# TensorE reads w1 through a register-held ring slot; q is scaled by VectorE

## The chip, the cores and the metric

One NeuronCore of a Trainium2 chip runs the kernel. The metric is the device time of one execution in microseconds. An execution counts as fast or slow by its state (a run over 1.5% above the fastest of the same kernel is slow); comparisons below use fast runs. A ratio is the mean time of one kernel's fast runs over the mean of the other's fast runs of the same rounds, with its 95% interval, so it is not quite the ratio of the medians that stand beside it.

Names of engines: PE is TensorE's array (PEld its weight loads, PEq or PEldq its sequencer), DVE is VectorE, ACT ScalarE, POOL GpSimd, SP the engine that issues most input and output transfers (128 of the 164 DMA issues on the page of the kernel before).

## The reference, cut to what matters

```python
# q, k, v: (8 batches, 8 heads, 576 tokens, 64); moe_w1: (8 experts, 512, 1024); moe_w2: (8, 1024, 512)
q_s = softmax(q, axis=-1)                      # per token: this is "q scaled"
k_s = softmax(k, axis=2)                       # over the tokens
x   = einsum(q_s, einsum(k_s, v))              # (8, 576, 512) after joining the heads
e_idx = argmax(x.mean(axis=1) @ w_gate)        # ONE expert for each batch
h   = maximum(x[b] @ w1[e_idx[b]], 0)
out[b] = gate_w[b] * (h @ w2[e_idx[b]])
```

For these inputs the gate chooses the experts 2, 3, 3, 1, 3, 3, 4, 6.

## The kernel before

The batches run one after the other. The expert's weights lie in SBUF in a ring of five slots, `w1_all` and `w2_all`. Batch b owns slot b mod 5. GpSimd loads the expert into that slot, unless one of the other slots already holds it. Which slot holds the weights of batch b is known only at run time (`sidx`). Before, VectorE reads that number into a register and copies the weights into the batch's own slot, so that PE's addresses are constants:

```python
def fetch(b, w_all, part):                     # once per half of w1 and of w2
    if "src" not in seqs[b]:
        seqs[b]["src"] = nc.values_load(seqs[b]["sidx"][0:1, 0:1], engines=[ET.DVE], ...)
    ...                                        # cs, fs: the half
    copy = nc.vector.tensor_copy(
        out=w_all[:, b % NS, cs, fs],
        in_=w_all[:, ds(seqs[b]["src"], 1), cs, fs].rearrange("p o c f -> p (o c) f"),
    )
def moe(b):
    w1_sb, w2_sb = w1_all[:, b % NS], w2_all[:, b % NS]
    for fc in range(NF):                       # 8 blocks of 128 rows of h
        for c in range(ND):                    # 4 matmuls of 512 tokens
            nc.tensor.matmul(phm, lhsT=w1_sb[:, c, fsl], rhs=xt[:, c, 0:SM], ...)
        for c in range(ND):                    # 4 matmuls of the last 64 tokens
            nc.tensor.matmul(pht[...], lhsT=w1_sb[:, c, fsl], rhs=xt[:, c, SM:S], ...)
        ...
        yield                                  # attention work of later batches is put in here
    ...                                        # w2 stage: 4 x 8 matmuls of 512 columns, 16 of 256
```

A "block" below is one turn of the `fc` loop: 8 weight loads and 8 matmuls. The w1 stage of a batch is eight blocks, the w2 stage follows. The attention work of the batches to come is put between the blocks, up to batch 6; batch 7 has none.

The softmax here doesn't subtract the row's maximum and nothing guards it: scores larger than these inputs give would overflow.

## Time and profile before

| | before |
|---|---|
| time, median of 3 runs | 215.05 us (213.42 to 219.71; the last counts as slow) |
| profiled span | 213.7 us, mean granted clock 0.919 |
| PE busy | 176.0 us (82%) |
| one block with nothing between (batch 7) | 0.98 us |

L181 is PE's transpose of the scaled q: of the 7.6 us that PE idles ahead of it, 3.0 are ended by GpSimd. L219 forms x; PE idles 2.7 us ahead of it.

### The profile page before, as it was taken

Reading aid. Unit: us, or ns where it says so; the run is one execution under the profiler, and the core shown is the slowest. Engines: PE = TensorE matmul, PEld = TensorE weight load, DVE = VectorE, ACT = ScalarE, POOL = GpSimd, SP = SyncE. Lnnn points to the kernel's source line nnn. Section 1 sums busy time; section 2 is a strip of 40 time slices with the busy share of each in tenths; the row PEclk is TensorE's granted clock in tenths of the full one; section 3 lists DMA queues with packets and bytes.
Section 4 is the critical chain, followed back from the end, with each engine's and each line's share of the span. In section 5 each row is a group of like instructions: output and inputs, shape, how many; then the busy total and the mean of one; then the engine's idle time right before and its main releaser. Section 6 shows DMA issues by size and latency. Waiting matters only on the chain.

```text
span 213.7 us, 4597 instructions
## 1 busy us (share of the span) xinstructions
PE 176.0 (82%) x1703; PEld 94.3 (44%) x1703; DVE 119.0 (56%) x365; ACT 113.3 (53%) x177; POOL 62.2 (29%) x70
## 2 busy tenths in 40 slices
PE   6357499996999379797498999999777979999990
PEld 6344345443545135433244454535343535545540
DVE  0757935137697977994455757974755365222000
ACT  2776854672974418651266728653582334546541
POOL 2143600630266330373026230730084302300000
PEclk9965559999999859999969999999996999999999
DMA  6999899999998998999999595814379751999044
GB/s 187 379 390 369 123 206 298 230 217 297 398 389 253 395 348 276 336 323 240 275 244 324 158 328 119 300 36 114 76 110 200 141 123 48 160 186 270 1 113 110
DMA packets 28582, 48.55 MB, mean 227 GB/s; under 512 B 2960, under 2 KB 10128, under 8 KB 28560
## 3 DMA queue, kind: packets, MB, share of 16 engines
q1 hardware_dynamic: 19472, 37.76, 53.5%
q0 software_dynamic: 8544, 10.49, 30.1%
q8 instruction: 13, 0.21, 0.4%
q10 hardware_dynamic: 544, 0.02, 0.1%
q14 instruction: 9, 0.07, 0.1%
HBM read 61.88 MB, written 9.44 MB: 334 GB/s over the span
## 4 chain that ended last, share of the span: by engine, by line
PE 43%; DMA 25%; DVE 19%; issue 5%; POOL 3%; ACT 1%; DVEq 1%; POOLq 0%; ACTq 0%
PE mm L421 19%; DMA w_all<-in_moe_w_dram 17%; PE mm L402 15%; DVE w_all L385 7%; DMA v_in<-in_v_dram 5%; DVE qs L142 4%; DMA wg_sb<-in_moe_w_gate_dram 3%; PE kv L160 2%; PE mm L436 2%; PE x L219 2%; PE ht L407 2%; DVE kv L170 2%; DVE qt L189 2%; DVE xt L230 1%; PE kv L181 1%
## 5 line engine op out<-in xcount | busy, mean ns | idle before, releaser
L402 PE MATMUL mm<-xt,w_all 128*128 128x512 f16 x256 | 69.9, 405 | 12.8 <-DVE w_all L385 12.8
L411 ACT ACTIVATE hsb<-mm 128x512 f16<-128x512 f32 x64 | 37.8, 596 | 45.0 <-PE mm L402 44.5
L421 PE MATMUL mm<-w_all,hsb 128*128 128x512 f16 x256 | 60.6, 383 | 0.4 <-DMA w_all<-in_moe_w_dram 0.3
L428 ACT ACTIVATE osb<-mm,gate 128x512 f32<-128x512 f32 x32 | 22.0, 687 | 37.3 <-PE mm L421 31.0
L385 DVE COPY w_all<-w_all 128x2048 f16 x28 | 29.5, 1052 | 14.0 <-DMA w_all<-in_moe_w_dram 13.7
L402 PEld LDWEIGHTS <-w_all 128*128 128x128 f16 x256 | 21.4, 102 | 34.8 <-DVE w_all L385 14.5
L145 POOL TENSOR_TENSOR eq<-eq,qsi 128x1152 f16<-128x1152 f16 x13 | 28.0, 2152 | 26.6 <-DVE qsi L144 25.5
L421 PEld LDWEIGHTS <-hsb 128*128 128x128 f16 x256 | 23.3, 98 | 26.2 <-issue 0.8
L230 DVE CUSTOM_DVE_ANT_0 xt<-x,ones_f 128x576 f16<-128x576 f32 x26 | 19.3, 743 | 17.1 <-PE x L220 17.1
L315 POOL DMA_DIRECT2D w_all<-in_moe_w_dram x18 | 8.2, 455 | 66.1 <-DMA w_all<-in_moe_w_dram 24.8
L142 DVE TENSOR_REDUCE qs<-eq 128x18 f32<-128x1152 f16 x16 | 21.5, 1343 | 10.1 <-ACT eq L124 10.1
L132 POOL CAST va<-v_in 128x1152 f16<-128x1152 f32 x14 | 17.7, 1261 | 24.7 <-DMA v_in<-in_v_dram 24.6
L407 PEld LDWEIGHTS <-w_all 128*128 128x128 f16 x256 | 17.0, 101 | 17.1 <-issue 3.3
L124 ACT ACTIVATE eq<-q_in 128x1152 f16<-128x1152 f32 x16 | 18.5, 1159 | 2.3 <-DMA q_in<-in_q_dram 2.3
L136 ACT ACTIVATE ek<-k_in 128x1152 f16<-128x1152 f32 x16 | 18.6, 1161 | 1.1 <-DMA k_in<-in_k_dram 1.1
L407 PE MATMUL ht<-xt,w_all 128*128 128x64 f16 x256 | 18.6, 197 | 0.0
L219 PE MATMUL x<-qt,kv 128*128 128x512 f16 x32 | 14.0, 438 | 2.7 <-DVE kv L170 0.8
L168 DVE RECIPROCAL icv<-kv 128x1 f32<-128x1 f32 x30 | 4.8, 162 | 18.7 <-PE kv L181 18.2
L160 PE MATMUL kv<-va,ek 64*128 64x129 f16 x270 | 11.7, 230 | 3.3 <-POOL va L132 2.1
L160 PEld LDWEIGHTS <-ek 64*128 64x128 f16 x288 | 10.1, 102 | 8.2 <-issue 6.6
L181 PE MATMUL kv<-ident,eq 64*128 64x64 f16 x270 | 7.3, 196 | 7.6 <-POOL eq L145 3.0
L170 DVE SCALAR_TENSOR_TENSOR kv<-kv,icv,blkmask 128x128 f16<-128x128 f32 x30 | 10.5, 351 | 1.1
(80 smaller groups left out, 133.8 us busy)
## 6 DMA issues: line engine op xcount, KB each, us to landing
w_all<-in_moe_w_dram POOLq DMA_DIRECT2D x30, 512.0 KB
q_in<-in_q_dram SPq DMA_DIRECT2D x16, 576.0 KB, 6.6
k_in<-in_k_dram SPq DMA_DIRECT2D x16, 576.0 KB, 9.2
v_in<-in_v_dram SPq DMA_DIRECT2D x16, 576.0 KB, 9.1
out_dram<-osb SPq DMA_DIRECT2D x64, 128.0 KB, 5.5
w_all<-in_moe_w_dram POOLq DMA_DIRECT2D x4, 256.0 KB
out_dram<-osb_t SPq DMA_DIRECT2D x16, 64.0 KB, 2.2
wg_sb<-in_moe_w_gate_dram ACTq DMA_DIRECT2D x2, 8.0 KB, 5.3
```

Of the source, the lines that this page charges most:

```text
L124: nc.scalar.activation(out=eq.rearrange("p j n d -> p n j d"), in_=ins.pop((n, "q")), func=AF.Exp)
L136: nc.scalar.activation(out=ek.rearrange("p j n d -> p n j d"), in_=ins.pop((n, "k")), func=AF.Exp)
L142: nc.vector.tensor_reduce(out=qs, in_=eq, op=ALU.add, axis=AX.X)
L145: eng.tensor_tensor(out=eq, in0=eq, in1=qsi.unsqueeze(3).to_broadcast([128, J, 2, Dh]), op=ALU.mult,)
L160: nc.tensor.matmul(kps[g][:, 0:129], lhsT=ek[r, j], rhs=va[r, j], start=(j == 0), stop=(j == J - 1),)
L230: nc.vector.tensor_tensor_reduce(out=xt[:, c, :], in0=px[:, 0:S], in1=ones_f32.to_broadcast([128, S]), scale=1.0, scalar=0.0, op0=ALU.mult ...
L385: copy = nc.vector.tensor_copy(out=w_all[:, b % NS, cs, fs], in_=w_all[:, ds(seqs[b]["src"], 1), cs, fs].rearrange("p o c f -> p (o c) f"),)
L402: nc.tensor.matmul(phm, lhsT=w1_sb[:, c, fsl], rhs=xt[:, c, 0:SM], start=(c == 0), stop=(c == ND - 1),)
L407: nc.tensor.matmul(pht[:, fc * ST:(fc + 1) * ST], lhsT=w1_sb[:, c, fsl], rhs=xt[:, c, SM:S], start=(fc == 0 and c == 0), stop=(fc == NF - ...
L411: nc.scalar.activation(out=hsb[:, fc, 0:SM], in_=phm, func=AF.Relu)
L421: nc.tensor.matmul(po, lhsT=hsb[:, fc, st * 128:st * 128 + 128], rhs=w2_sb[:, fc, :], start=(fc == 0), stop=(fc == NF - 1),)
L428: nc.scalar.mul(osb, po, gate)
```

## The change

The intent: PE takes w1 from whichever slot holds it, so the w1 copies and PE's waits for them go. The slot number sits in a PE register, and each weight load's address is worked out from it. Only w2 is still copied. The scaling of q moves to VectorE, which has lost half its copies. Cut to its core:

```diff
-            at(t - 4.25, scale_q, n, nc.gpsimd)
+            at(t - 3.25, scale_q, n, nc.vector)
...
+    def find(b):
+        seqs[b]["src"] = nc.values_load(seqs[b]["sidx"][0:1, 0:1], engines=[ET.PE], ...)
+
+    def w1_of(b, c, cols):
+        if b == 0:
+            return w1_all[:, 0, c, cols]
+        return w1_all[:, ds(seqs[b]["src"], 1), c, cols].rearrange("p o f -> p (o f)")
...
-                    phm, lhsT=w1_sb[:, c, fsl], rhs=xt[:, c, 0:SM],
+                    phm, lhsT=w1_of(b, c, fsl), rhs=xt[:, c, 0:SM],
...
-                    pht[...], lhsT=w1_sb[:, c, fsl], rhs=xt[:, c, SM:S],
+                    pht[...], lhsT=w1_of(b, c, fsl), rhs=xt[:, c, SM:S],
...
-            at(NU * b - 1 + 0.5 * part, fetch, b, w1_all, part)
-            at(NU * b + 4 + part, fetch, b, w2_all, part)
+        at(NU * b - 3, find, b)
+            at(NU * b + 4 + part, fetch, b, part)
-    places = [(15, 25), (30, 35), (41, 46), (58, 64), (74, 80), (91, 97)]
+    places = [(15, 25), (31, 36), (42, 47), (58, 64), (74, 80), (91, 97)]
```

A rule had to change with it: a batch that reuses an expert no longer holds w1 in its own slot, so it isn't entered in the list of slots to reuse. (That part of the diff is left out here.)

More of the change, by code (lines that the diff above doesn't have):

```diff
@@ L80 @@
     hist = consts.tile([1, 8], FP32)
-    nc.vector.memset(hist, -1.0)
+    nc.vector.memset(hist, 0.0)
     held = consts.tile([1, 8], FP16)
@@ L109 @@
     out_p = out.rearrange("b (p j) d -> b p j d", j=J)
-    ins, halves, seqs, issued, copies = {}, {}, {}, {}, {}
+    ins, halves, seqs, issued, uses = {}, {}, {}, {}, {}
     def load(n, names="qkv"):
@@ L278, in gate_step @@
             same = gat_pool.tile([1, 8], FP32, name="same")
-            nc.vector.tensor_tensor(
-                out=same, in0=hist, in1=eidx[0:1, 0:1].to_broadcast([1, 8]), op=ALU.is_equal
+            nc.vector.scalar_tensor_tensor(
+                out=same, in0=hist, scalar=-1.0, in1=eidx[0:1, 0:1].to_broadcast([1, 8]),
+                op0=ALU.add, op1=ALU.is_equal,
             )
@@ L291, in gate_step @@
             nc.vector.max_index(out=sidx, in_max=top, in_values=score)
-        nc.vector.tensor_copy(out=hist[:, slot:slot + 1], in_=eidx[0:1, 0:1])
+        if b:
+            loaded = gat_pool.tile([1, 1], FP32, name="loaded")
+            nc.vector.tensor_single_scalar(out=loaded, in_=top[:, 0:1], scalar=1.0, op=ALU.is_equal)
+            nc.vector.scalar_tensor_tensor(
+                out=hist[:, slot:slot + 1], in0=eidx[0:1, 0:1], scalar=1.0, in1=loaded,
+                op0=ALU.add, op1=ALU.mult,
+            )
+        else:
+            nc.vector.tensor_single_scalar(
+                out=hist[:, slot:slot + 1], in_=eidx[0:1, 0:1], scalar=1.0, op=ALU.add
+            )
         gone = (b + 2) % NS
-        nc.vector.memset(hist[:, gone:gone + 1], -1.0)
+        nc.vector.memset(hist[:, gone:gone + 1], 0.0)
         nmx = gat_pool.tile([1, 1], FP32, name="nmx")
@@ L321, in gate_step @@
         for load_inst in issued[b]:
-            for copy in copies.get(b - 1, ()):
-                apart(load_inst, copy)
+            for op in uses.get(b - 1, ()):
+                apart(load_inst, op)
     def apart(first, second):
@@ L372, in gate_spread, with fetch @@
         seqs[b]["gate"] = gate
-    def fetch(b, w_all, part):
-        if "src" not in seqs[b]:
-            seqs[b]["src"] = nc.values_load(
+    def find(b):
+        seqs[b]["src"] = nc.values_load(
+            seqs[b]["sidx"][0:1, 0:1], engines=[ET.PE], min_val=0, max_val=NS - 1,
+            skip_runtime_bounds_check_because=IN_RANGE,
+        )
+    def w1_of(b, c, cols):
+        if b == 0:
+            return w1_all[:, 0, c, cols]
+        return w1_all[:, ds(seqs[b]["src"], 1), c, cols].rearrange("p o f -> p (o f)")
+    def fetch(b, part):
+        if "dsrc" not in seqs[b]:
+            seqs[b]["dsrc"] = nc.values_load(
                 seqs[b]["sidx"][0:1, 0:1], engines=[ET.DVE], min_val=0, max_val=NS - 1,
@@ L380, in fetch, with use @@
             )
-        if w_all is w1_all:
-            cs, fs = slice(0, ND), slice(part * (F // 2), (part + 1) * (F // 2))
-        else:
-            cs, fs = slice(part * (NF // 2), (part + 1) * (NF // 2)), slice(0, D)
-        copy = nc.vector.tensor_copy(
-            out=w_all[:, b % NS, cs, fs],
-            in_=w_all[:, ds(seqs[b]["src"], 1), cs, fs].rearrange("p o c f -> p (o c) f"),
-        )
-        copies.setdefault(b, []).append(copy)
+        cs = slice(part * (NF // 2), (part + 1) * (NF // 2))
+        use(b, nc.vector.tensor_copy(
+            out=w2_all[:, b % NS, cs],
+            in_=w2_all[:, ds(seqs[b]["dsrc"], 1), cs].rearrange("p o c f -> p (o c) f"),
+        ))
+    def use(b, op):
+        uses.setdefault(b, []).append(op)
         for load_inst in issued.get(b + 1, ()):
-            apart(copy, load_inst)
+            apart(op, load_inst)
     def moe(b):
         xt = seqs[b]["xt"]
-        w1_sb, w2_sb = w1_all[:, b % NS], w2_all[:, b % NS]
+        w2_sb = w2_all[:, b % NS]
         hsb = h_pool.tile([128, NF, S], FP16, name="hsb")
@@ L401, in moe @@
             for c in range(ND):
-                nc.tensor.matmul(
-                    phm, lhsT=w1_sb[:, c, fsl], rhs=xt[:, c, 0:SM],
+                use(b, nc.tensor.matmul(
+                    phm, lhsT=w1_of(b, c, fsl), rhs=xt[:, c, 0:SM],
                     start=(c == 0), stop=(c == ND - 1),
-                )
+                ))
             for c in range(ND):
-                nc.tensor.matmul(
-                    pht[:, fc * ST:(fc + 1) * ST], lhsT=w1_sb[:, c, fsl], rhs=xt[:, c, SM:S],
+                use(b, nc.tensor.matmul(
+                    pht[:, fc * ST:(fc + 1) * ST], lhsT=w1_of(b, c, fsl), rhs=xt[:, c, SM:S],
                     start=(fc == 0 and c == 0), stop=(fc == NF - 1 and c == ND - 1),
-                )
+                ))
             nc.scalar.activation(out=hsb[:, fc, 0:SM], in_=phm, func=AF.Relu)
```

## The prediction

> **What bounds the kernel now.** I read the page of the profile first (busy shares, costliest groups), then TensorE's timeline, then the list of waits, then VectorE's and GpSimd's timelines at the points where TensorE stood idle.
>
> ```profile
> PE 176.0 (82%) x1703; PEld 94.3 (44%) x1703; DVE 119.0 (56%) x365; ACT 113.3 (53%) x177; POOL 62.2 (29%) x70
> L402 PE MATMUL mm<-xt,w_all 128*128 128x512 f16 x256 | 69.9, 405 | 12.8 <-DVE w_all L385 12.8
> L385 DVE COPY w_all<-w_all 128x2048 f16 x28 | 29.5, 1052 | 14.0 <-DMA w_all<-in_moe_w_dram 13.7
> ```
>
> TensorE is the bound: 176.0 of 213.7 us. Of its idle time, 12.8 us lies before the first w1 matmuls (L402) and is ended by the copy of w1 into the batch's own slot (L385), which the change removes. TensorE's timeline shows where:
>
> ```profile
> 51.03 1.04 PE L402 MATMUL mm<-xt,w_all 128*128 128x512 f16 x4 [1.84 <-DVE w_all L385]
> ...
> 75.96 1.89 PE L402 MATMUL mm<-xt,w_all 128*128 128x512 f16 x4 [4.79 <-DVE w_all L385]
> ...
> 105.89 1.04 PE L402 MATMUL mm<-xt,w_all 128*128 128x512 f16 x4 [2.74 <-DVE w_all L385]
> ...
> 128.61 1.04 PE L402 MATMUL mm<-xt,w_all 128*128 128x512 f16 x4 [0.47 <-DVE w_all L385]
> ...
> 151.14 1.04 PE L402 MATMUL mm<-xt,w_all 128*128 128x512 f16 x4 [1.47 <-DVE w_all L385]
> ...
> 176.41 1.04 PE L402 MATMUL mm<-xt,w_all 128*128 128x512 f16 x4 [1.47 <-DVE w_all L385]
> ```
>
> These are the starts of batches 1 to 6. Batch 7 starts at 192.84 without a wait. So each batch but the last pays one wait for the copy. Inside the w1 stage TensorE itself is dense where nothing is interleaved:
>
> ```profile
> 193.83 1.03 PE L402 MATMUL mm<-xt,w_all 128*128 128x512 f16 x4
> 194.70 0.28 PE L407 MATMUL ht<-xt,w_all 128*128 128x64 f16 x4
> 194.81 1.03 PE L402 MATMUL mm<-xt,w_all 128*128 128x512 f16 x4
> ```
>
> One block of 128 rows of h (4 matmuls of 512 columns, 4 of 64, 8 weight loads) takes 194.81 - 193.83 = 0.98 us; eight of them, 7.84 us, make the w1 stage. That is 16 instructions in 0.98 us, 61 ns each: little room for more work in TensorE's sequencer.
>
> [...] at 9.4 us 18 transposes with their weight loads start within about 0.25 us, some 7 ns per instruction. [...] the semaphore wait ahead of batch 7's first w1 weight load ran in the sequencer at 191.9 us, just when the 16 load-and-matmul pairs of L436 (32 instructions, from 191.85) began to run, and that repeats at 48.2, 127.1, 148.3 and 173.6 us. I take a run-ahead of 32 instructions. [...] a copy of half of w2 takes 0.69 us alone and 2.49 us at 59.21, while GpSimd scales q (58.59 to 61.15).
>
> **The change part by part.**
>
> *Removed copies.* 14 copies of half of w1 leave VectorE (0.71 us apiece when alone, 12.7 us in all by its timeline). On the path: in batches 1 and 3 the copy follows a late transfer, so 0.7 us each. In batches 4, 5 and 6 it follows the last piece of x: VectorE's piece ends at 127.87, 150.39 and 175.66, the first matmul starts 0.74 to 0.75 us later, so 0.7 us each. In batch 2 the copies sat in VectorE's queue until 73.3 and took 4.18 us for two because GpSimd was scaling q; x was there at 73.4, the matmul came at 75.96: 2.5 us. Sum 0.7 x 5 + 2.5 = 6 us.
>
> *q scaled on VectorE.* 12 of GpSimd's 13 scalings (2.15 us each) become VectorE's (1.36 us each by the three that it already does): +16.3 us on VectorE. With the copies gone and the w2 copies no longer stretched (16.9 us now, 14 x 0.7 = 10 us alone) VectorE stays near 119 us. TensorE's transposes now wait for GpSimd 3.0 us in all by the page; GpSimd's casts also stand behind fewer things, as at 158.4 to 161.7 where it did transfers, cast and scaling in a row. I give 2 us.
>
> *Register addresses.* The instruction order of the changed kernel has 896 more register operations on TensorE: one before every Ldweights and one before every Matmult of the w1 stage of batches 1 to 7, so 16 per block. No trace of TensorE has this operation. On VectorE the one ahead of each copy takes 67 ns, on GpSimd 50. Around it lies a further gap: GpSimd's skipped loads of batch 2 run 20 records, 16 of them register operations, from 71.24 to 73.05 us:
>
> ```profile
> L315 POOLq FUSED_REGOPS  x3: 42/50/62, 71.4 to 71.9; - x3
> L336 POOLq MOVE w_all<-in_moe_w_dram x2: 29/29/29, 72.4 to 72.8; - x2
> ```
>
> That is 1.8/20 = 91 ns apiece, gap included. So a block needs 16 x 91 = 1.46 us for register operations and 16 x 7 = 0.11 us for pushing its loads and matmuls: 1.6 us, an estimate, where TensorE's array needs 0.98. The w1 stage becomes limited by the sequencer: 8 x 1.6 = 12.8 us. Against this stands the run-ahead of 32 instructions, two blocks: up to 3.2 us are paid beforehand, if TensorE is busy or waiting long enough ahead of the stage; 1 us where it isn't (L436 lasts 1.0 us), 2 us typically with a wait of 1 us. And transposes and kv matmuls between the blocks give the sequencer time, less 0.5 us for pushing them.
> - Batch 1: 12.8 - 2 = 10.8 against 8.3: +2.5.
> - Batches 2 and 3: the stages take 14.8 and 12.0 now with interleaved work and waits: 0.
> - Batch 4: 12.8 + 0.5 - 2 = 11.3 against 10.1: +1.2.
> - Batch 5: 11.3 against 13.0 now, of which 2.5 are the GpSimd waits counted above: +0.8.
> - Batch 6: 10.8 against 8.4: +2.4.
> - Batch 7, with nothing ahead of it to wait for: 11.8 against 7.8: +4.
>
> Sum +10.9 us. The register load from SBUF on TensorE (0.3 us as on the others) stands three ticks earlier, under queued matmuls: nothing.
>
> *A load more.* The rule for reuse changes: a batch that reuses an expert no longer holds w1 in its own slot, so it doesn't enter the history. I worked out the gate's choices from the reference: experts 2 3 3 1 3 3 4 6. Before, batches 2, 4 and 5 reuse (the trace agrees: the four issues of these batches take 44 to 49 ns in place of 0.6 to 0.8 us). After, batch 5 finds slot 1 retired and loads again: 4.2 MB more of reads. Its issue falls near 134 us, where the DMA rate is 143 GB/s, 17 us ahead of use; w1 took 8.3 us at 180.4. Hidden.
>
> Total: 215 - 6 - 2 + 11 = 218, and about 1 us for what retimed waits cost (three gates come a tick later): 219 us.
>
> **The rivals.**
> 1. *Register operations are hidden.* If a block's 16 cost under 1.1 us (under 60 ns apiece), the run-ahead covers the stage, and the 8 us of gain remain: 207 us. For it: the array leaves 61 ns per instruction, the operation itself may be 50 ns. Against: the gap between sequencer records was never below 27 ns here.
> 2. [...]
> 3. *Waits change hands.* VectorE, now scaling q, delivers kv and x later, or the weights' transfer of batch 3 (20 us on the chain of waits) sets the end of stage 2 anyway: then the 2.5 us of batch 2 are not gained but waited for at batch 3. That makes 221 us.
>
> **Range and chances.** All hangs on the cost of a block: 1.1 us gives 207, 1.4 gives 213, 1.6 gives 219, 2.0 about 235 (five stages x 8 blocks x 0.4 us). I can't exclude the ends, so 205 to 242. Faster than 210.8: 0.30 (a block under 1.3 us, which whoever wrote this surely hoped for); within 2%: 0.25; slower: 0.45.
>
> **What would show it.** The changed profile should show register operations on TensorE's queue, their duration, and blocks of batch 7 at about 1.6 us in place of 0.98, with idle time before weight loads given as issue. If the blocks stay at 0.98, rival 1 holds[...]. The w2 stages should keep their 0.22 us per matmul. No matmul should wait for L385's successor at a batch's start; GpSimd should fall to about 36 us; batch 5's issues should take 0.6 us and software DMA move a quarter more. Wrong would be I if TensorE shows no such gaps, or if the time goes into the weights' transfers.

## More of the kernel before

The prediction shows the lines that carry the main argument, PE's waits for the w1 copies among them. Four more groups are needed later. They are from the costliest groups on the page of the kernel before; after the bar come the busy time, the mean ns of one, and the idle time of the engine just before them with what ended it.

```profile
L145 POOL TENSOR_TENSOR eq<-eq,qsi 128x1152 f16<-128x1152 f16 x13 | 28.0, 2152 | 26.6 <-DVE qsi L144 25.5
...
L407 PE MATMUL ht<-xt,w_all 128*128 128x64 f16 x256 | 18.6, 197 | 0.0
L219 PE MATMUL x<-qt,kv 128*128 128x512 f16 x32 | 14.0, 438 | 2.7 <-DVE kv L170 0.8
...
L181 PE MATMUL kv<-ident,eq 64*128 64x64 f16 x270 | 7.3, 196 | 7.6 <-POOL eq L145 3.0
```

The first row is the scaling of q on GpSimd.

## The result, and the profile after

The changed kernel takes 234.67 us (median of 4 runs, 234.63 to 236.1, all fast) against 215.28 us (4 runs): ratio 1.095 [1.086, 1.104]. It is slower by 9.5%.

The page of the changed kernel: busy times first, then the software DMA queue (packets, MB, share), then four groups.

```profile
PE 202.8 (87%) x1703; PEld 105.8 (45%) x1703; DVE 124.6 (53%) x370; ACT 115.4 (50%) x177; POOL 39.2 (17%) x58
...
q0 software_dynamic: 10144, 12.58, 33.2%
...
L426 PE MATMUL mm<-xt,w_all 128*128 128x512 f16 x256 | 69.1, 385 | 1.8 <-issue 0.2
...
L431 PE MATMUL ht<-xt,w_all 128*128 128x64 f16 x256 | 41.3, 191 | 6.2 <-issue 0.4
...
L145 DVE TENSOR_TENSOR eq<-eq,qsi 128x1152 f16<-128x1152 f16 x15 | 22.4, 1491 | 0.6
...
L406 DVE COPY w_all<-w_all 128x2048 f16 x14 | 14.9, 1067 | 8.3 <-DMA w_all<-in_moe_w_dram 7.8
```

The intent was met: the idle time ahead of the first w1 matmuls (now L426) fell from 12.8 to 1.8 us, and VectorE is no longer named there. But PE is "busy" 26.8 us more with the same 1703 matmuls. The row that grew is the small one: the 256 matmuls of 64 columns show 41.3 us where they showed 18.6, although each is as short as before (191 ns against 197). A row's busy time is the union of its pieces: matmuls that used to overlap (256 records of 50.4 us in all lay in 18.6 us) now come nearly one at a time (48.9 us in 41.3). PE's sequencer shows why. These are two rows of what lies on line L426 (count, then shortest, median and longest ns, then first and last start):

```profile
L426 PEldq FUSED_REGOPS  x448: 46/55/60, 47.9 to 219.0; - x150
...
L426 PEldq EVENT_SEMAPHORE  x9: 51/51/51, 28.1 to 205.0; - x9
```

448 register operations here and 448 more on L431 make 16 for each of the 56 blocks of batches 1 to 7. Half of them stand ahead of a weight load and half ahead of the matmul after it, whose row names `w_all` too (`mm<-xt,w_all`). The records of batch 7 put one beside the other (start in us, length in ns):

```
212.847  55  register operation
212.951  95  LDWEIGHTS
212.960  55  register operation
213.065 376  MATMUL
213.074  55  register operation
213.178  95  LDWEIGHTS
```

After the 55 ns of the record 49 ns more pass before the instruction starts, and the next register operation begins 9 ns after that: 113 ns for one register-addressed instruction. Sixteen make 1.81 us, and a block takes about 1.85 us. PE's timeline of batch 7 shows the blocks (start, length, idle before):

```profile
205.84 1.04 PE L426 MATMUL mm<-xt,w_all 128*128 128x512 f16 x4
206.72 0.31 PE L431 MATMUL ht<-xt,w_all 128*128 128x64 f16 x4
207.09 1.06 PE L426 MATMUL mm<-xt,w_all 128*128 128x512 f16 x4
208.00 0.87 PE L431 MATMUL ht<-xt,w_all 128*128 128x64 f16 x4
209.06 1.06 PE L426 MATMUL mm<-xt,w_all 128*128 128x512 f16 x4 [0.19 <-issue]
209.97 0.87 PE L431 MATMUL ht<-xt,w_all 128*128 128x64 f16 x4
210.94 1.06 PE L426 MATMUL mm<-xt,w_all 128*128 128x512 f16 x4
```

The first block still takes 1.25 us (207.09 - 205.84), because the sequencer had run ahead (its wait for this batch ran at 205.0, 0.84 us before the first matmul); the next take 1.97 and 1.88, where the kernel before had 0.98. The granted clock is 1.00 in this stretch, so it isn't the cause.

Stage by stage, from the first w1 matmul of a batch to that of the next (of batch 7, to its last matmul). The last column is one of the experiments and is used further down.

| batch | before | after | difference | after, half the register operations |
|---|---|---|---|---|
| 0 | 22.09 | 20.11 | -1.98 | 20.16 |
| 1 | 24.92 | 27.27 | +2.35 | 24.57 |
| 2 | 29.94 | 32.24 | +2.30 | 28.89 |
| 3 | 22.72 | 25.58 | +2.86 | 22.45 |
| 4 | 22.53 | 24.91 | +2.38 | 23.35 |
| 5 | 25.27 | 24.78 | -0.49 | 21.31 |
| 6 | 16.44 | 22.19 | +5.75 | 16.43 |
| 7 | 15.91 | 22.22 | +6.31 | 15.91 |
| sum | 179.82 | 199.30 | +19.48 | 173.07 |

The sum agrees with the spans (233.0 - 213.7 = 19.3). Batch 5's extra load, issued by GpSimd at 139.98, raised the software queue from 10.49 to 12.58 MB; no wait of PE names it.

One more loss shows in batch 2. PE's timeline, then VectorE's:

```profile
101.29 0.59 PE L219 MATMUL x<-qt,kv 128*128 128x512 f16 x1 [3.01 <-DVE pooled L230]
```

```profile
96.17 1.34 DVE L142 TENSOR_REDUCE qs<-eq 128x18 f32<-128x1152 f16 x1
97.55 0.27 DVE L144 RECIPROCAL qsi<-qs 128x18 f32<-128x18 f32 x1
97.85 2.72 DVE L145 TENSOR_TENSOR eq<-eq,qsi 128x1152 f16<-128x1152 f16 x1
100.49 0.74 DVE L230 CUSTOM_DVE_ANT_0 xt<-x,ones_f 128x576 f16<-128x576 f32 x1
```

PE waits 3.01 us for a 0.74 us copy of x, because the sum and the scaling of q stand ahead of it in VectorE's queue, 4.3 us of work; the scaling took 2.72 us there, twice the 1.36 us of VectorE's scalings in the kernel before.

### The profile page after: what moved, and what is told of

Same layout as the page of the kernel before. It is cut to its first block, busy times and chain, and to the rows that moved or that the text cites. A ratio compares the mean times of both kernels' runs of the same rounds, so it can differ in the third digit from the quotient of the medians.

```text
span 233.0 us, 5477 instructions
## 1 busy us (share of the span) xinstructions
PE 202.8 (87%) x1703; PEld 105.8 (45%) x1703; DVE 124.6 (53%) x370; ACT 115.4 (50%) x177; POOL 39.2 (17%) x58
## 3 DMA queue, kind: packets, MB, share of 16 engines
q0 software_dynamic: 10144, 12.58, 33.2%
## 4 chain that ended last, share of the span: by engine, by line
PE 67%; DVE 12%; DMA 8%; issue 5%; ACT 3%; SPq 1%; POOL 1%; DVEq 0%; ACTq 0%; POOLq 0%
PE mm L426 24%; PE mm L445 18%; PE ht L431 11%; DMA k_in<-in_k_dram 5%; PE kv L160 4%; PE x L219 3%; DMA v_in<-in_v_dram 3%; DVE eq L145 3%; PE mm L460 3%; DVE qs L142 2%; DVE kv L170 2%; DVE xt L230 2%; PE kv L181 2%; DVE qt L189 1%; ACT qt L187 1%
## 5 line engine op out<-in xcount | busy, mean ns | idle before, releaser
L426 PE MATMUL mm<-xt,w_all 128*128 128x512 f16 x256 | 69.1, 385 | 1.8 <-issue 0.2
L431 PE MATMUL ht<-xt,w_all 128*128 128x64 f16 x256 | 41.3, 191 | 6.2 <-issue 0.4
L431 PEld LDWEIGHTS <-w_all 128*128 (+1 forms) x256 | 22.8, 97 | 31.3 <-issue 6.2
L426 PEld LDWEIGHTS <-w_all 128*128 (+1 forms) x256 | 23.4, 98 | 29.7 <-issue 5.5
L327 POOL DMA_DIRECT2D w_all<-in_moe_w_dram x18 | 9.0, 501 | 114.1 <-DVE nmx L309 56.9
L145 DVE TENSOR_TENSOR eq<-eq,qsi 128x1152 f16<-128x1152 f16 x15 | 22.4, 1491 | 0.6
L406 DVE COPY w_all<-w_all 128x2048 f16 x14 | 14.9, 1067 | 8.3 <-DMA w_all<-in_moe_w_dram 7.8
L219 PE MATMUL x<-qt,kv 128*128 128x512 f16 x32 | 14.0, 436 | 5.8 <-DVE pooled L230 4.1
L160 PEld LDWEIGHTS <-ek 64*128 64x128 f16 x288 | 10.8, 108 | 8.0 <-issue 5.7
L160 PE MATMUL kv<-va,ek 64*128 64x129 f16 x270 | 12.7, 242 | 2.0 <-ACT qt L187 1.2
```

What stands on the lines that cost most here:

```text
L145: eng.tensor_tensor(out=eq, in0=eq, in1=qsi.unsqueeze(3).to_broadcast([128, J, 2, Dh]), op=ALU.mult,)
L160: nc.tensor.matmul(kps[g][:, 0:129], lhsT=ek[r, j], rhs=va[r, j], start=(j == 0), stop=(j == J - 1),)
L219: nc.tensor.matmul(px[:, 0:SM], lhsT=kvs[g], rhs=qts[g][:, 0:SM], start=True, stop=True)
L426: use(b, nc.tensor.matmul(phm, lhsT=w1_of(b, c, fsl), rhs=xt[:, c, 0:SM], start=(c == 0), stop=(c == ND - 1),))
L431: use(b, nc.tensor.matmul(pht[:, fc * ST:(fc + 1) * ST], lhsT=w1_of(b, c, fsl), rhs=xt[:, c, SM:S], start=(fc == 0 and c == 0), stop=(fc = ...
```

## The experiments

The medians of the table take in all runs of a kernel, the ratios fast runs alone. Where a run was slow, the median of the fast ones is: e1_static 207.32, e3_before_dve 215.92, e5_spin 294.93, e8_hybrid 213.66, e9_nr4 206.00, e10_w2reg 205.37, e11_spin3 209.77. The last two kernels to run, e11_spin3 and e12_nr4_pool, ran on another chip than the other ten; each ratio is to the kernel before in the same rounds.

Theory A: PE's sequencer is the bound of the w1 stages. A block takes the longer of the array's 0.98 us and the sum of the sequencer's times. Rival B: VectorE's queue, the added load and waits that changed hands. Rival C: a register-addressed load costs the array a fixed extra. Twelve kernels ran; all gave the reference's result. Those with slot numbers as constants are right for these inputs alone and serve as probes.

| run | median us | ratio to before |
|---|---|---|
| constant slots (e1_static) | 207.99 | 0.963 [0.951, 0.974] |
| half the register operations (e2_half) | 207.60 | 0.963 [0.954, 0.972] |
| before, q scaled by VectorE (e3_before_dve) | 215.93 | 1.000 [0.986, 1.013] |
| after, q scaled by GpSimd (e4_after_pool) | 232.65 | 1.080 [1.069, 1.091] |
| idle register operations, two per pair (e5_spin) | 295.01 | 1.359 [1.348, 1.370] |
| three quarters (e6_dose) | 214.05 | 0.992 [0.983, 1.000] |
| constant slots, q by GpSimd (e7_static_pool) | 211.32 | 0.974 [0.966, 0.982] |
| register in two blocks, q by GpSimd (e8_hybrid) | 213.90 | 0.984 [0.975, 0.993] |
| register in four blocks (e9_nr4) | 206.30 | 0.952 [0.944, 0.960] |
| the same, w2 by register (e10_w2reg) | 206.57 | 0.953 [0.944, 0.961] |
| idle register operations, one per pair (e11_spin3) | 211.06 | 0.966 [0.959, 0.973] |
| e9_nr4 with q by GpSimd (e12_nr4_pool) | 212.71 | 0.982 [0.976, 0.988] |

### No register operations: e1_static

```diff
-        if b == 0:
-            return w1_all[:, 0, c, cols]
-        return w1_all[:, ds(seqs[b]["src"], 1), c, cols].rearrange("p o f -> p (o f)")
+        return w1_all[:, [0, 1, 1, 3, 1, 0, 1, 2][b], c, cols]
...
-        at(NU * b - 3, find, b)
```

> The changed kernel, but PE reads w1 from slots that are constants in the program (the slots that the choices of these inputs give), so that no register operation stands before a w1 weight load or matmul; the result stays correct. Theory A (the register operations bound the w1 stages: about 113 ns for each register operation with its instruction, 32 of them, 1.85 us per block): blocks fall back to 0.98 us, the w1 stages lose some 25 to 30 us, the time falls to 203 to 209 us, below the kernel before, because the waits for w1 copies stay gone. Theory B (VectorE's queue, the reload of expert 3 and waits that changed hands make the loss): nothing of these is touched, the time stays at 228 to 236.

(The "32" in this text counts the 16 register operations and the 16 instructions that they serve.) Measured: 207.99 us. The whole loss goes with the register operations, and the time falls below the kernel before. Everything that rival B names, VectorE's added work, the added load and the retimed steps, is still in this kernel, so by itself B does not make the loss.

### Half of them: e2_half

```diff
-                    pht[...], lhsT=w1_of(b, c, fsl), rhs=xt[:, c, SM:S],
+                    pht[...], lhsT=w1_at(b, c, fsl), rhs=xt[:, c, SM:S],     # constant slot
```

> The changed kernel with only the 512-column matmuls of w1 addressed by the register, the 64-column ones by constants: half of the register operations, 16 per block in place of 32 counted with their instructions. Theory A in its form as a maximum (the sequencer's time and the array's time run beside each other, the longer one sets the block): 8 x 113 ns = 0.90 us plus 16 plain instructions, near the array's 0.98, so blocks of 1.0 to 1.2 us and 205 to 214 us. Theory C (each register-addressed weight load costs the array a fixed extra of about 0.055 us[...]): half of the excess stays, blocks of about 1.4 us, 218 to 223 us. Theory B: 228 to 236.

(The plain instructions that remain are 8 per block, not 16 as the text says.) Measured: 207.60 us, the same as with none. PE's timeline of batch 7:

```profile
185.92 1.04 PE L429 MATMUL mm<-xt,w_all 128*128 128x512 f16 x4
186.79 0.28 PE L434 MATMUL ht<-xt,w_all 128*128 128x64 f16 x4
186.91 1.03 PE L429 MATMUL mm<-xt,w_all 128*128 128x512 f16 x4
187.77 0.28 PE L434 MATMUL ht<-xt,w_all 128*128 128x64 f16 x4
187.89 1.03 PE L429 MATMUL mm<-xt,w_all 128*128 128x512 f16 x4
```

Blocks of 0.98 us (187.89 - 186.91), with 8 register operations in each: 8 x 113 ns = 0.90 us of sequencer time lie beside 0.98 us of array time and cost nothing. A fixed cost per register-addressed load (C) would have kept half of the excess. C falls.

### Three quarters: e6_dose

```diff
+    def w1_at(b, c, cols):                     # for the 64-column matmuls
+        if c < 2:
+            return w1_all[:, [0, 1, 1, 3, 1, 0, 1, 2][b], c, cols]
+        return w1_of(b, c, cols)
```

> Between half and all: the 512-column matmuls by register and, of the 64-column ones, two of four. 12 register operations per block in place of 8 (207.6 us) and 16 (234.7 us). Maximum of sequencer and array: 12 x 113 ns and 4 plain instructions make about 1.4 us against the array's 0.98, so about half of the changed kernel's loss: 217 to 224 us. A cost for each operation from the first one on would have shown at 8 already and would put this at 228 or so.

Measured: 214.05 us, below the expected range. The block was foreseen: batch 7's w1 stage takes 10.64 us, 1.33 per block, where 12 x 113 ns and 4 plain instructions gave 1.4. PE's timeline of batch 7 has them (190.36 to 191.74 is 1.38; the first ones are shorter by the run-ahead):

```profile
190.36 1.06 PE L431 MATMUL mm<-xt,w_all 128*128 128x512 f16 x4
191.26 0.45 PE L436 MATMUL ht<-xt,w_all 128*128 128x64 f16 x4
191.74 1.15 PE L431 MATMUL mm<-xt,w_all 128*128 128x512 f16 x4
```

What was too high was the share of it that reaches the end. Against the half dose, stage by stage as in the table above, batches 6 and 7 take 5.5 us more, but batches 1 to 5 together 1.4 us less: where attention work lies between the blocks, an excess of 0.35 us a block does not show. The shape is the one that a maximum gives: nothing at 8, 6.5 us at 12, 27 us at 16.

### Is it the operation or the address? e5_spin and e11_spin3

Constant slots again, with register operations that nobody needs ahead of each w1 pair of weight load and matmul (`SPIN` is 12 in the first kernel, which become two records per pair, and 3 in the second, which become one; the very last matmul of w1 takes its address from that register):

```diff
+    def spin(b):
+        for k in range(SPIN if b else 0):
+            nc.tensor.reg_mul(kept, kept, 1)
...
+                spin(b)
                 use(b, nc.tensor.matmul(phm, lhsT=w1_of(b, c, fsl), rhs=xt[:, c, 0:SM], ...))
```

> The run with constant slots (208 us), plus two register operations that nobody needs ahead of each w1 weight load and matmul pair of batches 1 to 7: 16 register operations per block as in the changed kernel, but the weight loads and matmuls keep constant addresses. Theory A1 (a register operation costs the sequencer its whole 105 ns, 55 of record and 50 of gap, wherever it stands): blocks of 1.8 to 1.9 us, 230 to 236 us. Theory A2 (only its 55 ns record is its own, and the gap of 50 ns is there because the next instruction takes its address from the result): 16 x 55 ns and 16 x 9 ns make about 1.0 us, blocks of 1.0 to 1.1, 207 to 214 us.

> The run with unneeded register operations again (295 us with 16 records per block, half of them 180 ns long), now with one short record of three multiplications ahead of each weight load and matmul pair: 8 per block, nothing addressed by a register. Theory A1 (sequencer time of record and gap, beside the array): 8 times some 110 to 130 ns make 0.9 to 1.05 us per block against the array's 0.98: 206 to 212 us, as the run with half of the register addresses. Rival (a register operation also stops the array, so that its time is added): blocks of 1.8 us, 230 us or more.

Measured: 295.01 and 211.06 us. The sequencer's rows, of the first kernel and then of the second:

```profile
L402 PEldq FUSED_REGOPS  x896: 32/174/188, 50.5 to 282.5; - x180
```

```profile
L402 PEldq FUSED_REGOPS  x448: 75/75/156, 48.9 to 195.9; - x150
```

The 295 us lie far outside both ranges: I had counted records and not how long they are. The twelve multiplications of a pair became one record of 180 ns and one of 32 ns (how they are shared out isn't shown), and behind each stands a gap of some 60 ns, so that one pair takes 348 ns in the records (54.056 to 54.404 us for the start of one to that of the next). Eight pairs make 2.78 us, and batch 7's w1 stage of 22.16 us is 2.77 per block. In the second kernel a pair takes 153 ns from record to record, eight make 1.23 us, and batch 7's 9.58 us are 1.20 per block. So theory A1 holds in kind: a record and the gap behind it take the sequencer's time even where no address depends on it, and the block is the larger of the two sums. A2, under which the gap belongs to the address, leaves only the records and 9 ns for each instruction: with the lengths measured, 8 x 230 ns = 1.84 us per block for the first kernel and 8 x 93 ns = 0.74 us, hidden under 0.98, for the second. Both blocks are longer (2.77 and 1.20), so A2 falls; its "207 to 214 us" rested on records of 55 ns and says nothing. The rival of the second text, that the array stops too, would have made 1.8 us or more of the 1.20.

The 295 us also hold a lower clock. The same columns for a stretch of batch 7 in the changed kernel and then in the first of these two (the stretch, its length, busy times of five engines, then the granted PE clock, the DMA share and GB/s):

```profile
206.00:220.00 14.00, 12.50 (x64) 5.80 (x63) 0.00 (x0) 5.12 (x9) 0.00 (x0) 1.00 0.15 34
```

```profile
262.00:282.00 20.00, 16.42 (x57) 6.45 (x57) 0.00 (x0) 3.97 (x7) 0.00 (x0) 0.65 0.08 17
```

With 0.98 us of array work in 1.85 us the clock stays at 1.00; with 0.98 in 2.77 its mean is 0.65. The w1 blocks don't feel it, as they wait for the sequencer (eight pairs of 348 ns fill the 2.77 us), but the w2 stage of batch 7 lasts 9.10 us in place of 8.06. Of these two stretches the sparser has the lower clock; no run here separates the share of busy time from other causes. (This profile fell in a slow run; the fast runs of the same kernel have a mean granted clock of 0.767 to 0.794, those of the changed kernel 0.937 to 0.946.)

### q scaled by the other engine: e3_before_dve, e4_after_pool, e7_static_pool

Each is one line, `scale_q` at t - 3.25 on VectorE against t - 4.25 on GpSimd, in the kernel before, in the changed kernel, and with constant slots.

> The kernel before with q scaled by VectorE in place of GpSimd (this part of the change alone). If the two parts add: 211 to 215 us (the prediction put this part at minus 2). If VectorE's in-order queue is what suffers (rival B), the w1 copies and pooled copies of x come later and the time rises to 217 to 223.

> The changed kernel with q scaled by GpSimd again (the register addressing alone). Theory A: the w1 stages stay at 14 to 16 us, the time at 230 to 238. Rival B (VectorE's queue is the loss): PE's waits for the pooled copies of batches 2 and 3 go, and the time falls by 5 us or more, to below 229.

> Constant slots with q scaled by GpSimd again: what the scaling by VectorE costs once PE is not bound by register operations. If its 2 us (234.7 against 232.7) are a wait of its own: 205 to 207 us, and the second-layer stages of batches 1 and 2 shorten from 14 to 12 us. If they came only from the shift of PE's stages: 208 as with VectorE.

Measured: in the kernel before nothing (215.93 us, ratio 1.000, whose interval leaves room for some 3 us either way); the changed kernel gets faster with GpSimd (232.65 against 234.67 us), and the one with constant slots slower (fast medians 211.32 against 207.32). In neither pair do the fast runs overlap, but the two kernels of a pair ran in different rounds and the intervals of their ratios overlap, so each sign is likely and its size rough. The first lay between the two expectations. The last was a miss in sign: I expected 205 to 208. The rows of PE say what is exchanged. Of the kernel before with VectorE (compare the 2.7 and 7.6 us shown of the kernel before):

```profile
L219 PE MATMUL x<-qt,kv 128*128 128x512 f16 x32 | 14.0, 438 | 5.9 <-DVE pooled L230 2.9 <-DVE gate L371 1.3 <-DVE kv L170 0.8
...
L181 PE MATMUL kv<-ident,eq 64*128 64x64 f16 x270 | 8.0, 205 | 4.3 <-DVE eq L145 2.5 <-DVE kv L170 1.6 <-DVE gt L357 0.3
```

The 3.3 us that PE's transposes no longer wait for GpSimd come back as 3.2 us of waits ahead of L219 for VectorE, which has q in its queue. Now the changed kernel, with VectorE and then with GpSimd:

```profile
L219 PE MATMUL x<-qt,kv 128*128 128x512 f16 x32 | 14.0, 436 | 5.8 <-DVE pooled L230 4.1 <-DVE kv L170 0.7 <-ACT xt L224 0.7
...
L181 PE MATMUL kv<-ident,eq 64*128 64x64 f16 x270 | 7.5, 199 | 4.0 <-DVE eq L145 2.2 <-DVE kv L170 1.6 <-DVE gt L369 0.3
```

```profile
L219 PE MATMUL x<-qt,kv 128*128 128x512 f16 x32 | 13.7, 429 | 2.4 <-DVE kv L170 0.8 <-ACT xt L224 0.7 <-DVE pooled L230 0.5
...
L181 PE MATMUL kv<-ident,eq 64*128 64x64 f16 x270 | 7.2, 196 | 5.3 <-DVE eq L145 2.5 <-DVE kv L170 1.6 <-POOL eq L145 1.0
```

GpSimd's 1.0 us here is a third of the 3.0 of the kernel before. A likely reason, which no run tests, is that the slower w1 stages leave GpSimd time to be done, so that VectorE has little to win and its queue to lose. Rival B therefore holds for some 2 us of the loss, not for the 5 or more that the text asked of it.

### For any input: e8_hybrid, e9_nr4, e12_nr4_pool

If 8 register operations per block are free, the register may be used as long as no block has more. In e9_nr4 the 512-column matmuls of blocks 0 to 3 read by the register, and their 64-column matmuls are moved into blocks 4 to 7, whose own weights are a copy in the batch's slot. Only half of w1 is copied, and the copy has four blocks of time:

```diff
+    NR = 4
+        if b == 0 or fc >= NR:
+            return w1_all[:, b % NS, c, cols]            # own slot: copied
+        return w1_all[:, ds(seqs[b]["src"], 1), c, cols].rearrange("p o f -> p (o f)")
...
+            if fc >= NR or not b:
+                for c in range(ND):
+                    if tails:                             # 64-column matmuls of blocks 0 to NR - 1
+                        tail(*tails.pop(0))
+                    tail(fc, c)
...
+        at(NU * b - 0.5, fetch, b, w1_all, 0)            # columns NR * 128 to 1023
```

e8_hybrid has NR = 2, two copies of 384 columns, q scaled by GpSimd and the `places` of the kernel before. e12_nr4_pool is e9_nr4 with q scaled by GpSimd.

> A version for any input that tries to beat both kernels: only the first two blocks of each w1 stage are addressed by the register, the 512-column matmuls at once and their 64-column ones strewn among the later blocks, so that no block has more than 8 register operations; the later blocks read copies that VectorE makes meanwhile (three quarters of the w1 copies of before); q scaled by GpSimd. Theory A: blocks stay at 0.98 to 1.0 us, no wait for copies at the start of a stage: 204 to 209 us. If VectorE's copies, or the placing, bring new waits: 210 to 215.

> For any input: the 512-column matmuls of the first four blocks by the register, their 64-column ones put into the last four blocks, so that each of the eight blocks has 8 register operations (free in the run with half of them); only columns 512 to 1023 of w1 are copied, one VectorE copy per batch with four blocks of slack; q scaled by VectorE. Theory A: as the run with half the register operations, 206 to 210 us. If the first hybrid's 213.9 us came from VectorE's and GpSimd's attention work and not from PE's waits for copies: 211 to 215.

> The best kernel so far (206.3 us) with q scaled by GpSimd: the second part of the change alone, now where nothing else binds PE. By the pair with constant slots (208.0 with VectorE, 211.3 with GpSimd): 208 to 212 us. If the two are equal here as in the kernel before: 205 to 208.

Measured: 213.90, 206.30 and 212.71 us. The first missed its expectation for the reason that its rival names: its last two w1 stages take 8.52 and 7.85 us, so the blocks are right, and the time is lost in batches 1 to 5. The third run says that the scaling of q is enough to explain it: it has the four blocks and GpSimd and is nearly as slow (a little over its expected range). Two blocks with VectorE were not run, so a share of the number of blocks, the copies or the `places` isn't excluded. PE's rows for the second and the third kernel:

```profile
L448 PE MATMUL mm<-xt,w_all 128*128 128x512 f16 x256 | 65.3, 389 | 2.3 <-DMA w_all<-in_moe_w_dram 2.3
...
L220 PE MATMUL x<-qt,kv 128*128 128x512 f16 x32 | 13.8, 431 | 5.8 <-DVE pooled L231 3.0 <-DVE gate L384 1.3 <-DVE kv L171 0.8
...
L182 PE MATMUL kv<-ident,eq 64*128 64x64 f16 x270 | 7.4, 198 | 4.0 <-DVE eq L146 2.1 <-DVE kv L171 1.6 <-DVE gt L370 0.2
```

```profile
L448 PE MATMUL mm<-xt,w_all 128*128 128x512 f16 x256 | 66.7, 395 | 4.2 <-DMA w_all<-in_moe_w_dram 4.0 <-ACT hsb L457 0.2
...
L220 PE MATMUL x<-qt,kv 128*128 128x512 f16 x32 | 14.0, 438 | 2.3 <-DVE kv L171 0.8 <-ACT xt L225 0.7 <-DVE pooled L231 0.5
...
L182 PE MATMUL kv<-ident,eq 64*128 64x64 f16 x270 | 7.5, 199 | 9.3 <-POOL eq L146 5.7 <-DVE eq L146 1.8 <-DVE kv L171 1.6
```

The same exchange as before, but with PE fast, GpSimd's 5.7 us weigh more than VectorE's 2.5 more at L220. Waits are not the whole of it. In the same work of batch 5 (the end of w1, the start of w2) the granted clock (the third figure from the end) is 1.00 in e9_nr4, where PE had waited 1.15 us for GpSimd shortly before, and 0.58 in e12_nr4_pool, where it had waited 1.45 and 1.37 us:

```profile
154.00:160.00 6.00, 4.93 (x63) 2.72 (x63) 5.38 (x12) 3.52 (x5) 1.69 (x2) 1.00 1.12 192
```

```profile
159.00:165.00 6.00, 6.00 (x26) 2.56 (x25) 3.86 (x11) 2.56 (x4) 2.12 (x1) 0.58 1.01 168
```

No run separates the waits from the clock that goes with them. No wait for a copy of w1 is left in e9_nr4; what PE now waits for ahead of w1 is the transfer of the weights themselves, in batch 3:

```profile
102.00 1.87 PE L448 MATMUL mm<-xt,w_all 128*128 128x512 f16 x4 [2.26 <-DMA w_all<-in_moe_w_dram]
```

e9_nr4 beats both kernels: 0.952 [0.944, 0.960] of the kernel before.

### w2 by register too: e10_w2reg

```diff
-                    po, lhsT=hsb[...], rhs=w2_sb[:, fc, :],
+                    po, lhsT=hsb[...], rhs=w2_of(b, fc, slice(0, D)),   # ds(seqs[b]["src"], 1)
...
-                    po[64 * dh:64 * dh + 64, 0:HD], lhsT=hsb[:, fc, SM:S], rhs=...   # 16 of 256 columns
+                    po[0:64, :], lhsT=hsb[:, fc, SM:S], rhs=w2_of(b, fc, slice(0, D))  # 8 of 512
...
-            at(NU * b + 4 + part, fetch, b, w2_all, part)
```

The last matmuls take another form in this run, which writes all its output from partition 0 on.

> The same, and PE reads w2 too by the register (it is the moving operand, so only the matmul needs a register operation, one of about 113 ns against 216 ns of array time), so that VectorE's 14 w2 copies (14.9 us) go. Theory A: the register operations lie beside the array, the second-layer stages stay at 8.1 us in the last two batches, and the freed VectorE time shows in batches 1 and 2: 202 to 207 us. If a register-addressed moving operand costs more than its share (a matmul that can't start until the operation is done, with nothing ahead of it): last stages of 9 us and more, 212 or above.

Measured: 206.57 us, in the range for A and no better than e9_nr4. PE's timeline of batch 7 (its profile fell in a slow run, so only pieces within it are compared):

```profile
193.14 7.07 PE L471 MATMUL mm<-w_all,hsb 128*128 x32
200.14 1.91 PE L484 MATMUL mm<-w_all,hsb 128*64 x8
```

The 32 matmuls take the same 7.07 us as in the changed kernel with constant w2 addresses: one 113 ns operation per 216 ns matmul is free. The stage is nevertheless 8.92 us long because of the new form of the last matmuls, 1.91 us in place of 1.06. So "8.1 us" failed for a reason that isn't the register's. VectorE's busy time falls from 126.9 to 114.0 us; no gain of time is seen. Whether the w2 copies were on the path stays open, as the new form costs 0.85 us in a stage where nothing hides it and may cover a gain.

## Why the prediction was right or wrong

The direction, the most likely class and the range (205 to 242) held. The point, 219.0 us, was 15.7 us too low, and nearly all of that is one term of the sum, the register addresses. That the range held is in part luck: by its own scale of 0.4 us a block for 16 us, a block of 1.85 us gives 229; the rest came from what the prediction thought hidden.

**Removed copies, -6 us: right.** Constant slots with q still on GpSimd (e7_static_pool) have the removed copies alone, apart from the retimed steps and the added load, and give 0.974 [0.966, 0.982], which is 5.7 us (4 to 7) of 216.3. The place of the gain was less well foreseen: in its profile batch 3 starts 5.0 us earlier (100.93 against 105.89), after a wait of 4.07 us for the transfer of its weights, and loses 3.1 us of that again within its own stage.

**q on VectorE, -2 us: likely the wrong sign in this kernel.** The prediction counted the 3.0 us of PE's waits for GpSimd; that VectorE's queue would pass them on stands in its third rival, but not in its sum. Alone it gave 0, give or take 3 us; in the changed kernel the medians with and without it differ by 2 us the other way. Where PE is fast it does win: 4 us by the fast medians of e7_static_pool and e1_static, and, with intervals that don't overlap, 7 us by those of e12_nr4_pool and e9_nr4. VectorE did not stay near 119 us but reached 124.6, as the w2 copies took 14.9 us and not 10.

**Register addresses, +10.9 us: mis-sized.** Half of the operations cost nothing, so the last two columns of the stage table show what they cost in the changed kernel: 199.30 - 173.07 = 26.2 us. The step was right in its mechanism (the sequencer becomes the bound, about 16 operations per block) and failed in three of its sizes:
- *1.6 us per block.* It took 91 ns an operation from GpSimd's sequencer and 7 ns for the instruction. On PE it is 104 and 9, and a block takes 1.85 us. That is 0.25 x 8 = 2 us for each stage that it bounds.
- *A run-ahead of two blocks, 2 us where a wait stands ahead.* The run-ahead in instructions was right: batch 7's semaphore wait ran at 205.0 us, as the 32 instructions of the last w2 matmuls had begun at 204.84. But that is only the 1.0 us that those take, and the further 1 us was to come from PE's wait for the copy, which the same change removes. It was in effect counted as a gain twice. Batch 6's w1 stage took 14.19 us against 8 x 1.85 = 14.8, so 0.6 us were saved, not 2; batch 7 (14.16 us) saved 0.6 and not 1.
- *"Batches 2 and 3: 0".* The work and the waits between their blocks were thought to hide it. Against the half dose they lost 3.4 and 3.1 us, part of the first with the wait of 3.01 us for VectorE shown above.

In batches 6 and 7, where nothing else interferes, the first two account for the miss: 12.1 us against the predicted 6.4; 4.0 from the block and 1.8 from the run-ahead make 5.8 of the 5.7 missing. In batches 1, 4 and 5 the terms can't be told apart from what the attention work hides.

One reading went wrong on the way: "16 instructions in 0.98 us, 61 ns each: little room" divides the array's time. By the prediction's own 7 ns an instruction the sequencer is busy for 0.11 us of the 0.98, and e2_half puts 0.90 us of register-addressed instructions into the same 0.98.

**The load more: hidden, as predicted.** e1_static and e2_half carry it too, are the faster kernels, and have PE wait for a transfer of weights only near 41 and 102 us, not in batch 5. (The 143 GB/s is the mean of the stage from 128.6 to 151.1 us, not the rate at 134. And the software queue moved a fifth more, 12.58 against 10.49 MB, not a quarter: six loads in place of five.) **"About 1 us for retimed waits"** was not tested by itself.

**The rivals.** "Register operations are hidden" is true of 8 per block and false of 16. Blocks take 0.98 us with 8 register-addressed instructions and 1.85 with 16, and a gap of some 60 ns stands behind a register operation with no address involved too (e5_spin, e11_spin3). "The weights' transfer of batch 3 sets the end of stage 2 anyway" is false of the changed kernel, whose batch 3 begins at 108.39 without a wait, and true of the fast ones: e9_nr4 waits 2.26 us for it and begins at 102.00 (e2_half 1.42 us).

## What to carry to other kernels

In this kernel a dynamic address on PE cost sequencer time for each instruction that names it, the matmul as well as its weight load. Put the sum per block (113 ns each here) beside the array's time per block, and spread the addressed instructions so that the first stays below the second: in e2_half and e9_nr4 they then cost nothing that shows. Don't credit a saving that the change itself takes away, as the run-ahead during a wait that it removes. And a step moved to an idle-looking engine hands its wait to whatever stands behind it in that engine's queue (in batch 2 of the changed kernel a 0.74 us copy behind 4.3 us of work, for which PE waited 3.01 us): the same move was worth about 0, -4, -7 or +2 us in four kernels that differ in what bound PE.
